# Row statistics in stages, row loads two steps ahead, left q and k in SBUF, and routing over two steps, in a recurrent attention kernel with a routed MLP

## The chip, the cores and the metric

One core of one Trainium2 chip. The metric is the device time of one execution in microseconds (us); a time below is the median of several executions. One execution of each kernel was profiled, and stage lengths come from those profiles. The profiled execution of the kernel before was long (span 2297.4 us, its median is near 2287). Steps 1 to 61, the steady steps, differ from profile to profile. Six profiles of kernels in which these steps are those of the kernel before (before, b_stats, b_qkl, b_both, b_tail, b_dn128) spread from 1974.6 to 2001.7 us, mean 1988.5; three with those of the changed kernel (after, a_again, a_route) from 1919.3 to 1941.6, mean 1929.6. The profile of the kernel before is the longest of its six, so I give the mean beside it where it matters, and read nothing from a difference under some 27 us between two profiles' steady steps.

## The reference, cut to what matters

```python
xn = layernorm(x)                       # x: [1, 2048, 1024] bf16
# A: 64 segments of 32 rows; 8 memory rows go from one segment to the next
for s in range(64):
    h = concat([mem, xn[:, 32*s:32*s+32]])           # 40 rows
    q, k, v = h @ Wq, h @ Wk, h @ Wv                 # 32 heads of 128
    o = softmax(mask(q @ k.T * scale)) @ v @ Wo
    mem = o[:, :8]; outs.append(o[:, 8:])            # recurrence
# B: the 2 rows with the largest xn @ w_r get a gated MLP (F = 3584)
r = xn @ w_r; idx = argsort(-r)[:, :2]
y = (silu(xn[idx] @ w_gate) * (xn[idx] @ w_up)) @ w_down * sigmoid(r[idx])
return x + A + (xn + scatter(y))
```

The four projections have 64 granules of 512 KB. 42 stay in SBUF; 22 must be read again in each of the 64 steps, since each segment needs the memory rows of the one before.

## The kernel before

The row statistics (mean, root of the variance) of all 2048 rows and the router sums are made during step 0, one tile of 128 rows after another. `hook(p, kc, fn)` puts a piece of work after chunk kc of phase p of a step; the phases are the six half projections (q0, k0, q1, k1, v0, v1).

```python
psT = tile_pool(name="psT", bufs=1, space=PSUM)        # ONE buffer, tag "t"
PHASES = [(0, 0), (1, 0), (0, 1), (1, 1), (2, 0), (2, 1)]
...
def stats(t):                                          # one tile in one go
    RI[t] = row_stats(pro, xt(t), P, MS[:, t, 0:1], MS[:, t, 1:2])   # DVE, Sqrt on ACT, DVE
    XN[t] = ...
    nc.gpsimd.tensor_scalar(XN[t], xt(t), MS[:, t, 0:1], subtract)
    nc.scalar.activation(XN[t], XN[t], Copy, scale=RI[t])
def router(t):                                         # DVE product with WB, sum into R
    ...
    if t == NT - 1: nc.vector.tensor_copy(out=RB, in_=R)   # frees the memory of the statistics
...
def norm(X, XN, PS, n):                                # normalize the rows of the next segment
    SC = one.tile([P, 2], F32, tag="sc", name="SC")
    nc.vector.tensor_copy(out=SC[0:n, :], in_=PS[0:n, :])  # PS is a tile of psT
    ...
def transposes(mat, half, XB):
    PTq = psT.tile([P, 4, 4, 32], BF16, tag="t", name="PTq")   # needs the same buffer
    ...
def left_keys(half):                                   # q, k of the 8 left rows, by way of HBM
    QKL[half] = load_qkl(0, half) if s == 0 else QKLs.pop(0)
...
hook(1, 1, load_rows(s + 1)); hook(3, 1, norm_rows(s + 1)); hook(4, 4, rows_st)
if s == 0:
    for t in range(1, NT): hook(*divmod(2*t - 1, 8), stats(t))
    for t in range(NT):    hook(*divmod(2*t + 1, 8), router(t))
if s == NSEG - 1:                                      # all routing in the last step
    for k, fn in zip(((0,0), (1,6), (2,0), (3,0), (4,0)), routed): hook(*k, fn)
hook(2, 5, scores(0)); hook(4, 5, scores(1))
# transposes of (q,1) come at (3, 3): two chunks after norm_rows at (3, 1)
...
# w_down: 16 loads of 2 x 112 rows, so 112 partitions each
```

## Time and profile before

| | us |
|---|---|
| median of the first 3 runs | 2284.81 (2281.93 to 2290.77) |
| profiled span | 2297.4 |
| step 0 | 138.7 |
| steps 1 to 61 | 2001.7 (32.8 each) |
| step 62, step 63 | 30.3, 46.4 |
| gate, up, down, end | 80.3 |

The stages end where ScalarE evicts the projection of a step.

### The profile page before, as it was taken

The numbers are of one execution on the slowest core, as the hardware profiler recorded it, in microseconds if no ns is written. First come the engines' busy times: TensorE is split into PE (matmuls) and PEld (weight loads), VectorE is DVE, ScalarE is ACT, GpSimd is POOL, SyncE is SP. The second block draws the span as 40 slices with busy tenths as digits, with TensorE's granted clock in tenths as the row PEclk, the third lists the DMA queues.
The fourth block names the chain that finished last, engine by engine and source line by source line (L and its number), as shares of the span: only waits on it lengthen the run. The fifth ranks groups of instructions, "written<-read, shape, count | busy, mean of one in ns | idle before, by whom it ended". The sixth has DMA issues, their size and how long they took to land.

```text
span 2297.4 us, 81760 instructions
## 1 busy us (share of the span) xinstructions
PE 1784.4 (78%) x36210; PEld 918.3 (40%) x36210; DVE 751.0 (33%) x2223; ACT 484.6 (21%) x1116; POOL 562.1 (24%) x1039
## 2 busy tenths in 40 slices
PE   2378788888888878888878888878878888887754
PEld 1134344344434444444444434444443444444321
DVE  6523233332333233323322332333223323332220
ACT  2222122212222222222212221222222122222120
POOL 6421312222131212222131222213122222222110
PEclk8589899999999899899998998898998999999967
DMA  9699999999999999999999999999999999999977
GB/s 364 213 351 388 347 363 350 379 372 364 363 357 389 347 365 368 368 372 365 380 368 361 355 376 346 370 384 350 370 348 339 387 356 388 368 374 356 382 274 232
DMA packets 294291, 818.35 MB, mean 356 GB/s; under 512 B 37520, under 2 KB 42672, under 8 KB 293936
## 3 DMA queue, kind: packets, MB, share of 16 engines
q1 hardware_dynamic: 267680, 782.33, 92.0%
q0 software_dynamic: 23936, 26.33, 3.5%
q8 instruction: 283, 4.64, 0.8%
q10 hardware_dynamic: 2320, 4.46, 0.5%
q14 instruction: 72, 0.59, 0.1%
HBM read 800.35 MB, written 12.59 MB: 354 GB/s over the span
## 4 chain that ended last, share of the span: by engine, by line
PE 41%; DMA 31%; DVE 11%; issue 8%; ACT 5%; POOL 1%; ACTq 0%; POOLq 0%; DVEq 0%; SPq 0%
PE PSm L538 19%; DMA g<-in_A_Wq_dram 16%; DMA g<-in_A_Wo_dram 6%; PE WO L576 5%; PE PSl L542 4%; DMA qkl_d<-QS 3%; PE PTq L403 3%; PE WL L576 2%; DVE SPS L450 2%; DVE NM L449 2%; ACT VM L560 2%; PE OP L490 1%; DMA g<-in_A_Wk_dram 1%; PE SPS L444 1%; ACT SPS L451 1%
## 5 line engine op out<-in xcount | busy, mean ns | idle before, releaser
L538 PE MATMUL PSm<-wres,ST 128*32 128x512 bf16 x8192 | 784.8, 419 | 20.8 <-DVE ST L298 17.9
L538 PE MATMUL PSm<-g,ST 128*32 128x512 bf16 x4096 | 443.0, 417 | 76.7 <-DMA g<-in_A_Wq_dram 53.7
L538 PEld LDWEIGHTS <-ST 128*32 128x32 bf16 x12288 | 314.4, 100 | 448.7 <-issue 210.0
L550 ACT CAST XB<-PSm 128x512 bf16<-128x512 f32 x256 | 150.2, 587 | 634.0 <-PE PSm L538 598.4
L576 PEld LDWEIGHTS <-OT 128*32 128x32 bf16 x8192 | 212.7, 98 | 78.9 <-issue 61.6
L576 PE MATMUL WO<-wres,OT 128*32 128x256 bf16 x5120 | 231.0, 278 | 12.3 <-issue 10.3
L403 PE MATMUL PTq<-IDENT,XB 128*128 128x128 bf16 x1024 | 109.0, 234 | 151.9 <-DVE SC L248 96.9
L542 PE MATMUL PSl<-wres,STL 128*32 128x512 bf16 x2048 | 215.1, 408 | 0.0
L323 POOL DMA_DIRECT2D QKL<-qkl_d x128 | 93.4, 729 | 383.2 <-PE SPS L444 155.5
L576 PE MATMUL WO<-g,OT 128*32 128x256 bf16 x3072 | 160.0, 277 | 33.9 <-DMA g<-in_A_Wo_dram 21.7
L403 PEld LDWEIGHTS <-XB 128*128 128x128 bf16 x1024 | 68.0, 102 | 258.7 <-ACT XB L550 130.5
L432 POOL COPY KT<-QKL 128x128 bf16<-128x128 bf16 x128 | 38.0, 297 | 538.6 <-PE WO L576 401.4
L609 POOL DMA_DIRECT2D out_dram<-OB x256 | 131.2, 518 | 74.6 <-DVE OB L605 35.6
L451 ACT ACTIVATE SPS<-SPS 128x320 f32<-128x320 f32 x128 | 54.0, 422 | 425.7 <-DVE SPS L450 338.6
L495 ACT CAST OT<-OP 128x256 bf16<-128x256 f32 x256 | 95.3, 372 | 209.7 <-PE OP L492 209.7
L408 DVE COPY QT<-PTq 128x512 bf16<-128x512 bf16 x128 | 53.7, 420 | 261.5 <-PE PTq L403 261.5
L490 PE MATMUL OP<-PT,VM 32*128 32x40 bf16 x2048 | 94.2, 178 | 49.9 <-ACT VM L560 45.8
L410 DVE COPY KT<-PTq 128x512 bf16<-128x512 bf16 x128 | 54.3, 424 | 208.5 <-PE PTq L403 205.6
L490 PEld LDWEIGHTS <-VM 32*128 32x128 bf16 x2048 | 65.4, 91 | 139.1 <-ACT VM L560 83.0
L497 DVE CAST OTL<-OP 128x64 bf16<-128x64 f32 x128 | 28.8, 225 | 270.1 <-ACT OT L495 270.1
L542 PEld LDWEIGHTS <-STL 128*32 128x32 bf16 x3072 | 87.2, 102 | 71.3 <-issue 21.8
L449 DVE TENSOR_REDUCE NM<-SPS 128x8 f32<-128x320 f32 x128 | 62.9, 492 | 158.7 <-PE SPS L444 158.7
(127 smaller groups left out, 2021.0 us busy)
## 6 DMA issues: line engine op xcount, KB each, us to landing
g<-in_A_Wq_dram SPq DMA_DIRECT2D x384, 512.0 KB, 7.0
g<-in_A_Wo_dram SPq DMA_DIRECT2D x384, 512.0 KB, 5.7
g<-in_A_Wk_dram SPq DMA_DIRECT2D x320, 512.0 KB, 7.2
g<-in_A_Wv_dram SPq DMA_DIRECT2D x320, 512.0 KB, 7.7
qkl_d<-QS POOLq DMA_DIRECT2D x64, 128.0 KB, 5.7
QKL<-qkl_d POOLq DMA_DIRECT2D x128, 64.0 KB, 5.8
g<-in_B_w_gate_dram SPq DMA_DIRECT2D x16, 448.0 KB, 6.0
g<-in_B_w_up_dram SPq DMA_DIRECT2D x16, 448.0 KB, 5.9
```

Source lines behind the costliest of these rows:

```text
L323: nc.gpsimd.dma_start(out=t[:, :, :], in_=qkl_d[s // 4][:, half, :, s % 4, :].rearrange("m p c -> p m c"))
L403: nc.tensor.transpose(out=PTq[:, il, :, :].rearrange("p j r -> p (j r)"), in_=XB[:, il * P:(il + 1) * P], identity=IDENT[:, :])
L410: nc.vector.tensor_copy(out=keys(half)[:, :, 0:32], in_=pv)
L449: nc.vector.tensor_reduce(out=NM[:, :], in_=S8, axis=AX.X, op=ALU.max, negate=True)
L451: nc.scalar.activation(out=S8, in_=S8, func=ACTF.Exp, scale=SCALE)
L490: nc.tensor.matmul(o, lhsT=VM[half][q0:q0 + 32, il * P:(il + 1) * P], rhs=PTm[q0:q0 + 32, il, 0:NK], start=True, stop=False, tile_position ...
L495: nc.scalar.copy(out=OT[half][:, 2 * ph:2 * ph + 2, :, :], in_=ov[:, :, :, 0:SEG])
L538: nc.tensor.matmul(PSm[32 * jq:32 * jq + 32, :], lhsT=ST[:, kc, :], rhs=Gv[:, 512 * jq:512 * (jq + 1)], start=(kc == 0), stop=(kc == KC - ...
L542: nc.tensor.matmul(PSl[32 * jq:32 * jq + 32, :], lhsT=cur["stl"][:, kc, :], rhs=Gv[:, 512 * jq:512 * (jq + 1)], start=(kc == 0), stop=(kc ...
L550: nc.scalar.copy(out=XB[:, :], in_=PSm[:, :])
L576: nc.tensor.matmul(PS[32 * g:32 * g + 32, 0:256], lhsT=lhs(h), rhs=Gv[:, D * hs + 256 * g:D * hs + 256 * (g + 1)], start=(first and hs == ...
L609: nc.gpsimd.dma_start(out=out2[s * SEG:s * SEG + XM, 256 * g:256 * (g + 1)], in_=OB[32 * g:32 * g + XM, 0:256])
```

## The change

Its intent: keep VectorE's queue flowing in step 0, so that the memory of the statistics comes free sooner; move the normalization of the next segment's rows from (3,1) to (0,4), which needs the rows loaded two steps ahead; spare the first segment's round trip of left q and k through HBM; take the router's search out of the last step; and load w_down in 128 partitions.

```diff
-    def stats(t): ...
+    def stats_a(t): ...     # DVE moments
+    def stats_b(t): ...     # Sqrt on ACT, reciprocal, subtraction on GpSimd
+    def stats_c(t): ...     # scaling on ACT, next load of x
@@ step 0
-            for t in range(1, NT):
-                hook(*divmod(2 * t - 1, 8), lambda t=t: stats(t))
             for t in range(NT):
-                hook(*divmod(2 * t + 1, 8), lambda t=t: router(t))
+                for fn, d in ((stats_a, 0), (stats_b, 1), (stats_c, 3), (router, 4)):
+                    if t > 0 or fn is router:
+                        hook(*divmod(max(2 * t - 2, 0) + d, 8), lambda t=t, fn=fn: fn(t))
@@ every step
-            hook(1, 1, ahead("x", lambda s=s: load_rows(s + 1)))
-            hook(3, 1, ahead("xn", lambda X, s=s: norm_rows(s + 1, X), "x"))
-            hook(4, 4, ahead("st", rows_st, "xn"))
+            hook(0, 4, ahead("xn", lambda s=s, X=XX[1]: norm_rows(s + 1, X)))
+            hook(1, 0, ahead("st", rows_st, "xn"))
...
+        if s + 2 < NSEG:
+            XX.append(load_rows(s + 2))            # after the residual of step s
...
-        hook(5, 2, lambda: attend(0, 0))
-        hook(5, 5, lambda: attend(0, 1))
+        hook(5, 3, lambda: attend(0, 0))
+        hook(5, 6, lambda: attend(0, 1))
@@ left q, k of step 0
+                nc.gpsimd.tensor_copy(out=first_left(half)[:, mat, :]..., in_=QS[:, 0, :, :])
...
-            QKL[half] = load_qkl(0, half) if s == 0 else QKLs.pop(0)
+            if s > 0:
+                QKL[half] = QKLs.pop(0)
@@ routing
-            for k, fn in zip(((0, 0), (1, 6), (2, 0), (3, 0), (4, 0)), routed):
-                hook(*k, fn)
+        if s == NSEG - 2:
+            hook(0, 0, routed_a); hook(3, 5, routed_b); hook(4, 0, routed_c)
+        if s == NSEG - 1:
+            hook(0, 6, routed_d); hook(2, 2, routed_e)
@@ w_down
-                nc.sync.dma_start(out=t[0:FK, :]..., in_=B_w_down[2 * what[1] * FK:(2 * what[1] + 2) * FK, :]...)
+                nc.sync.dma_start(out=t..., in_=B_w_down[2 * what[1] * P:(2 * what[1] + 2) * P, :]...)
```

Cut here: some loads of step 0 go from GpSimd's to ScalarE's queue; the hooks of the left rows move by a few chunks; routing keeps its data in one stream slot instead of two and takes the sigmoid from an exponential; silu and product of the MLP are cut in blocks of 128.

## The prediction

> **What bounds the kernel now.** I cut the run into stages first. A step is one of the 64 segments; it ends with the eviction of the projection (L604). The view of busy time by stretches, with step 0, steps 1 to 61, step 62, step 63, then gate and up, down, and the end (columns: PE, PEld, DVE, ACT, POOL busy, granted clock, DMA share, GB/s):
>
> ```profile
> 0.00:138.70 138.70, 51.27 (x692) 21.13 (x692) 71.89 (x179) 34.66 (x57) 62.50 (x60) 0.71 0.79 290
> 138.70:2140.40 2001.70, 1643.73 (x34225) 857.25 (x34225) 648.12 (x1964) 430.74 (x1021) 480.58 (x942) 0.93 0.99 366
> 2140.40:2170.70 30.30, 22.99 (x475) 11.49 (x475) 9.41 (x29) 6.17 (x16) 5.24 (x11) 0.94 1.03 404
> 2170.70:2217.10 46.40, 30.02 (x550) 16.03 (x554) 16.13 (x39) 10.33 (x21) 4.69 (x11) 0.74 0.75 255
> 2217.10:2255.20 38.10, 17.00 (x200) 5.86 (x192) 2.12 (x8) 2.75 (x5) 8.12 (x15) 0.58 0.94 359
> 2255.20:2280.00 24.80, 17.40 (x68) 5.92 (x68) 0.81 (x2) 0.00 (x0) 0.00 (x0) 0.89 1.05 282
> 2280.00:2297.40 17.40, 2.01 (x8) 0.58 (x7) 2.48 (x2) 0.00 (x0) 0.97 (x2) 0.63 0.01 2
> ```
>
> The reader is to see one bound, the weight stream: in 2002 us of steady steps the 16 DMA engines are busy 0.99 of the time, and a step takes 2001.7 / 61 = 32.8 us because 22 granules of 512 KB have to come in. Only where the share drops is there time to win: step 0 lacks 0.21 x 138.7 = 29 us of transfer time, step 63 lacks 0.25 x 46.4 = 11.6, gate and up 0.06 x 38.1 = 2.3, the end 17. The down stage is different: fully busy, yet slow.
>
> The same view inside step 0 shows where its stream stands still, and SyncE's own timeline and the chain of waits say why:
>
> ```profile
> 75.00:85.00 10.00, 6.26 (x82) 2.12 (x81) 3.25 (x9) 4.13 (x4) 3.21 (x3) 0.61 0.38 91
> 90.00:105.00 15.00, 6.02 (x56) 2.24 (x56) 12.25 (x27) 5.57 (x10) 9.19 (x4) 0.61 0.16 61
> 115.00:125.00 10.00, 4.24 (x73) 1.66 (x72) 1.48 (x3) 2.25 (x4) 2.44 (x4) 0.56 0.53 175
> ```
> ```profile
> SPq L204 <- DVE RB L159: 11.1, 1, 11.1
> ```
> ```profile
> 105.14 4.08 DMA qkl_d<-QS
> ...
> 110.20 6.19 DMA qkl_d<-QS
> ...
> 116.95 3.32 DMA QKL<-qkl_d
> ...
> 127.73 9.97 DMA wres<-in_A_Wo_dram
> ```
>
> The resident projection weights reuse the memory of the row statistics, so their loads wait for the last router sum (RB, at 105.7 us): DVE is the bound until then. After it, the first left q and k make a round trip through HBM (105 to 120 us) while PE stands.
>
> Step 63, by its timeline:
>
> ```profile
> 2182.99 2.28 DVE L342 MAX8 V<-g 1x8 f32<-1x2048 bf16 x1 [6.29 <-DMA g<-r_d]
> ...
> 2188.03 0.23 PE L439 MATMUL SPS<-KT,QT 128*32 128x40 bf16 x4 [5.45 <-DVE KT L410]
> ...
> 2198.51 0.34 PE L360 MATMUL PXS<-IDENT,g 2*128 2x2 bf16 x8 [5.09 <-DVE QT L408]
> ```
>
> The whole routing chain sits in this step. DVE waits 6.29 us for a DMA, searches for 2.28 + 2.27 us, and PE waits 5.45 and 5.09 us behind it. From the table of waits, the one that all steps share (total, times, longest):
>
> ```profile
> PE PTq L403 <- DVE SC L248: 96.9, 62, 3.8
> ```
>
> [...] The before kernel loads w_down in 112 partitions[...]. The trace has the effect: in the down stage 282 GB/s in 2 KB runs, beside 391 in a stretch with the Wo loads, which have the same 2 KB runs over 128 partitions (below). [...] the router product takes 2.01 us beside GpSimd's subtraction and 1.21 us without[...].
>
> ```profile
> DMA packets 3536, 6.77 MB, mean 282 GB/s; under 512 B 238, under 2 KB 238, under 8 KB 3535
> ```
> ```profile
> DMA packets 2400, 5.86 MB, mean 391 GB/s; under 512 B 207, under 2 KB 207, under 8 KB 2398
> ```
>
> **The change part by part.**
>
> Statistics in stages. No instruction goes away. A tile still costs DVE 1.28 (bn_stats, two) + 0.21 + 0.16 + 0.15 + 0.16 + about 2.0 (router), 4.0 us with overlaps, and the clean stretch from 25 to 40 us already runs one tile per 4.05 us. So staging doesn't speed up a tile. It removes the stalls between tiles, where DVE waited for a square root queued on ScalarE behind the scaling of a tile that GpSimd had not finished. By stretches, DVE is busy about 60 us of the 82 between 23.7 and 105.7; 22 are idle. Some idleness stays (the softmax of half 0 waits for PE and two table loads, and the square root still follows a scaling): I keep 10. The first matmul starts perhaps 1 us earlier, from 23.3, because x rows no longer queue behind mem0 on GpSimd. RB then comes at about 105.7 - 12 - 1 = 93 us.
>
> First left q and k in SBUF. Adds four GpSimd copies of some 0.3 us (the like KT copy takes 0.297), removes four round trips; the two that stalled PE cost 12.1 us (scores 0) and 9.5 us (scores 1). After RB, step 0 is then set by 15 projection granules: 7.9 MB at 375 GB/s = 21 us, plus landing and last matmuls, some 4 us. Step 0 ends near 93 + 25 = 118 instead of 138.7: **-20 us**. The two parts aren't added; the round trip lies inside that 33 us tail after RB.
>
> Routing over two steps. Step 63 loses the two DMA hops, both searches and the waits on them; it keeps a short normalization of two rows and, with the exponential in place of the sigmoid, one table load less. It should fall from 46.4 to the 32.8 to 34 of a streamed step. Step 62 takes on the search, 4.55 us of DVE, some 1 us of it seen by PE, and one stream slot of six is held for two steps instead of two for one: I give 30.3 -> 31.5. Sum: **-12 us**.
>
> Row loads two steps ahead, rows normalized at (0,4). This moves the SC wait, 96.9 / 62 = 1.56 us per step, to a place where DVE is free; the later attend hooks cut some of the 0.9 us waits on VM. PE gains up to 2 us per step, but the stream sets the step. With 0.01 of 2002 us of share to win, 20 us at most, I take half: **-10 us**. This is the least certain term.
>
> Tail. Later hooks end the 4.9 us that PE waited for the last XL rows: gate and up **-3 us**. Down in 14 loads of 128 partitions: 7.34 MB / 282 GB/s = 26.0 us becomes 7.34 / 385 = 19.1: **-7 us**. Four silus and four products in place of two each add about 1 us at the joint, beside six prefetched granules, so nothing. The last 17.4 us stay.
>
> Sum: -20 - 12 - 10 - 3 - 7 = -52; 2284.8 - 52 = **2233 us**.
>
> **Rivals.** (a) The freed waits come back as waits on the stream in all steps, as the share of 0.99 suggests: the steady term is 0, total 2243. (b) DVE's rate rules step 0: 4.05 us x 16 tiles plus the softmax leaves RB near 100, step 0 saves 12; total 2241, with (a) 2251. For it: DVE is 4.7 of 5 us busy in clean stretches. Against: the 22 idle us. (c) The steady steps are partly PE-bound: in every fourth step PE shows almost no wait for weights, and is busy 28 of 32.7 us. Then 1.5 us come off in 16 to 32 steps, another -15 to -30: 2205 to 2220. (d) The slot held for two steps starves steps 62 and 63, or the search shifts its stall into step 62: +5 to +8. (e) w_down is slow for another reason than the 112 partitions: +7.
>
> **Range and chances.** Step 0 is good to about 8 us, the steady steps to 12, the tail and routing to 5 each; together some 16, so 2212 to 2255 for 8 in 10. A gain over 2% means below 2240, 7 us from my centre: 0.63 for faster, 0.36 for same, 0.01 for slower.
>
> **What would show it.** Step 0 ending at 114 to 124 us, RB at 90 to 97, no HBM trip before the first scores; step 63 at 32 to 36 us with a share above 0.95; down near 19 us at over 370 GB/s; the SC wait nearly gone, and waits for weights up by part of it. I am wrong if RB is still after 100, if the steady steps move by over 25 us in all either way, or if step 62 grows by over 4 us.

Its sum is -20 - 12 - 10 - 3 - 7 = -52 us, so 2233 us. Moving loads from GpSimd's to ScalarE's queue is given no gain; no run tested that alone. "The effect" is that of the 112 partitions, which the prediction took for the cause without a run that showed it; b_dn128 below is that run. Each of the 8 loads of an activation table takes 1.28 us in the trace. Its 375 and 385 GB/s (the views have 366, 391 and 404) and its allowances of 4 us for landing and last matmuls and 1 us for the smaller blocks are my estimates.

## More of the kernel before

One line of the page carries what the stage table hides: the granted TensorE clock, in tenths of full speed, over 40 equal slices of the span.

```profile
PEclk8589899999999899899998998898998999999967
```

The clock reads 8 in some slices and 9 in others, all along the steady steps. A 9 means 90% or more; worked out exactly, the 34 slices that lie wholly in these steps have 0.87 to 1.00, and only two of them 1.00, so nearly every slice ran in part at half clock. Busy time at half clock is longer for the same matmuls: in a row of 128x512 matmuls the fourth after a given one starts 216 ns later at a clock of 1.00 and 427 ns later at 0.50 (medians, steps 1 to 61). So "busy" isn't a fixed amount of work here.

## The result

The changed kernel takes **2187.57 us** (median of 4 runs, 2176.01 to 2196.95), the kernel before 2286.97 us (4 runs, 2281.93 to 2290.77). The ratio is 0.9564, 95% interval 0.9514 to 0.9615, so about 99 us or 4.4% faster. A ratio is the mean time of one kernel's fast runs over the mean of the other's fast runs of the same rounds, so it is not quite the ratio of the medians. The forecast was 2233 us, a gain of 52, with a range from 2212: the direction is right, the size is outside the range.

The view of busy time by stretches, changed kernel, with the same stages and columns as the first fence of the prediction:

```profile
0.00:123.20 123.20, 50.81 (x692) 21.21 (x692) 66.91 (x179) 34.38 (x57) 57.95 (x54) 0.72 0.90 326
123.20:2064.80 1941.60, 1599.50 (x34225) 842.50 (x34225) 650.77 (x1964) 426.42 (x1021) 481.36 (x941) 0.96 1.01 378
2064.80:2094.90 30.10, 22.15 (x476) 11.24 (x476) 14.15 (x33) 6.06 (x15) 7.00 (x15) 1.00 1.00 371
2094.90:2127.00 32.10, 23.48 (x550) 13.33 (x554) 11.92 (x38) 9.03 (x20) 2.56 (x7) 1.00 1.03 402
2127.00:2160.50 33.50, 18.16 (x197) 5.52 (x188) 1.67 (x8) 2.88 (x7) 8.08 (x15) 0.62 0.99 385
2160.50:2179.00 18.50, 15.18 (x65) 5.14 (x65) 1.68 (x5) 0.00 (x0) 0.00 (x0) 0.85 1.03 392
2179.00:2195.40 16.40, 1.96 (x8) 0.49 (x6) 2.48 (x2) 0.00 (x0) 0.97 (x2) 0.62 0.01 3
```

The reader is to look at the second line. TensorE does the same 34225 matmuls as before, but in 1599.5 instead of 1643.7 us, at a mean clock of 0.96 instead of 0.93, and the stage takes 60 us less. The DMA share, 0.99 before, is now 1.01.

| stage | before | after | difference | forecast |
|---|---|---|---|---|
| step 0 | 138.7 | 123.2 | -15.5 | -20 |
| steps 1 to 61 | 2001.7 | 1941.6 | **-60.1** | **-10** |
| steps 62 + 63 | 76.7 | 62.2 | -14.5 | -12 |
| after the steps | 80.3 | 68.4 | -11.9 | -10 |

Three of four terms are near. The whole error lies in the steady steps; their difference is 59 us between the means of six and of three profiles too. Of the waits there, the tables of waits say (whole run, changed kernel; total, times, longest):

```profile
PE PTq L420 <- ACT XB L572: 67.2, 82, 6.7
...
PE PTq L432 <- DVE QT L425: 21.5, 16, 2.5
```

The wait for SC (96.9 us before) is gone, but others have grown: in steps 1 to 61 the wait for XB from 14 to 51 us, the wait for QT from 5 to 32 and the waits for weights from 87 to 111. In all, TensorE waits 330 us in these steps where it waited 349. The 19 us don't make 60. The rest is on the other side of its account: busy time fell by 44 us for the same matmuls. So the clock has to be read.

This is the view of busy time by four neighbouring stretches of 3.41 us in step 2 of the kernel before; the last three columns are the granted clock, DMA share and GB/s:

```profile
178.48:181.89 3.41, 3.41 (x85) 1.58 (x77) 1.03 (x3) 0.18 (x1) 0.96 (x2) 1.00 1.02 402
181.89:185.30 3.41, 1.20 (x21) 0.66 (x21) 3.00 (x11) 0.75 (x2) 0.08 (x1) 1.00 1.03 365
185.30:188.71 3.41, 3.41 (x31) 1.09 (x24) 0.53 (x2) 1.09 (x2) 1.22 (x2) 0.50 1.00 377
188.71:192.12 3.41, 3.20 (x75) 1.36 (x72) 1.77 (x4) 0.25 (x1) 0.71 (x1) 1.00 0.95 335
```

In the second stretch TensorE is busy for only 1.20 us, because it waits 2.21 us for SC. VectorE is busy 3.00 us of it: with the softmax of half 0 and with an eviction, behind which the small copy stands in its queue. Its timeline ends so:

```profile
184.08 0.65 DVE L554 CAST XBl<-PSl 128x512 bf16<-128x512 f32 x1
184.66 0.14 DVE L248 COPY SC<-PS 96x2 f32<-96x2 f32 x1
```

In the third stretch the clock is 0.50, and 31 matmuls fill the time in which 85 and 75 ran in the first and fourth (their mix differs somewhat). A wait of 2.2 us goes on costing after it is over: at half clock, 3.41 us hold the work of 1.7, as the 427 and 216 ns above say.

In steps 1 to 61 the kernel before has 66 such intervals of half clock, most of 3.41 us, together 272 us (266 if the one that began before is left out, as in the expectations below). For 36 of them (130 us) some of a wait for SC lies in the 3.41 us before they begin. The changed kernel has 35, together 138 us (133), none of them after such a wait. Only clocks of 0.5 and 1.0 occur in the trace, in multiples of 3.413 us but for the last interval of the run. By the 427 and 216 ns an interval at 0.5 loses half of its length: 272 x 0.5 less 138 x 0.5 is an estimate of 67 us, beside the 60 measured. That closeness is partly luck, since 272 is the highest of the six profiles (160 to 272, mean 211; the changed kernel's three have 116 to 138, mean 125). With the means the estimate is 43 of 59 us. All executions, profiled or not, say much the same: each lists its granted clock, and time x (1 - clock), the time lost to the throttle in the whole run, averages 182 us over 24 executions of the kernel before (clock 0.913 to 0.930; its profile has 0.907) and 122 us over the 10 of the changed kernel. So some 60 of the 99 to 102 us of the whole change, and some 40 of the 60 in the steady steps, are clock by this estimate.

What comes before such an interval can be counted too. Of the 65 that begin in steps 1 to 61 of the kernel before, 63 follow 3.41 us in which no single pause of TensorE reached 2.4 us; the longest pause had a median of 1.4 us. TensorE was busy for 1.69 us of those 3.41 in the median, and never for more than 2.04. In these steps of the two profiles (before, after) I cut the full-clock intervals into stretches of 3.41 us: all 20 with under 1.4 us of busy time were followed by half clock, 79 of the 170 with 1.4 to 2.2 us, and none of the 844 with 2.2 us or more.

### The profile page after: what moved, and what is told of

Same layout as the page of the kernel before. It is cut to its first block, busy times and chain, and to the rows that moved or that the text cites. A ratio compares the mean times of both kernels' runs of the same rounds, so it can differ in the third digit from the quotient of the medians.

```text
span 2195.4 us, 81816 instructions
## 1 busy us (share of the span) xinstructions
PE 1731.2 (79%) x36202; PEld 899.4 (41%) x36202; DVE 749.6 (34%) x2229; ACT 478.8 (22%) x1117; POOL 557.9 (25%) x1032
## 4 chain that ended last, share of the span: by engine, by line
PE 41%; DMA 37%; DVE 8%; issue 7%; ACT 3%; POOL 2%; ACTq 0%; SPq 0%; POOLq 0%; DVEq 0%
PE PSm L560 18%; DMA g<-in_A_Wo_dram 12%; DMA g<-in_A_Wq_dram 7%; PE WO L600 6%; PE PSl L564 6%; DMA g<-in_A_Wv_dram 5%; DMA qkl_d<-QS 5%; PE WL L600 2%; PE PTq L420 2%; DMA XL<-in_A_x_dram 2%; PE OP L509 1%; DMA QKL<-qkl_d 1%; DVE SPS L469 1%; DVE NM L468 1%; PE PTq L432 1%
## 5 line engine op out<-in xcount | busy, mean ns | idle before, releaser
L560 PE MATMUL PSm<-wres,ST 128*32 128x512 bf16 x8192 | 754.9, 398 | 23.1 <-DVE ST L300 17.8
L560 PE MATMUL PSm<-g,ST 128*32 128x512 bf16 x4096 | 421.9, 398 | 70.1 <-DMA g<-in_A_Wk_dram 31.8
L560 PEld LDWEIGHTS <-ST 128*32 128x32 bf16 x12288 | 301.2, 98 | 409.1 <-issue 164.7
L420 PE MATMUL PTq<-IDENT,XB 128*128 128x128 bf16 x1024 | 103.6, 225 | 81.1 <-ACT XB L572 67.2
L420 PEld LDWEIGHTS <-XB 128*128 128x128 bf16 x1024 | 60.2, 99 | 185.6 <-ACT XB L572 161.4
L516 DVE CAST OTL<-OP 128x64 bf16<-128x64 f32 x128 | 28.8, 225 | 284.5 <-ACT OT L514 284.5
L564 PE MATMUL PSl<-g,STL 128*32 128x512 bf16 x1024 | 106.2, 403 | 0.0
```

The source lines that it names most:

```text
L420: nc.tensor.transpose(out=PTq[:, il, :, :].rearrange("p j r -> p (j r)"), in_=XB[:, il * P:(il + 1) * P], identity=IDENT[:, :])
L560: nc.tensor.matmul(PSm[32 * jq:32 * jq + 32, :], lhsT=ST[:, kc, :], rhs=Gv[:, 512 * jq:512 * (jq + 1)], start=(kc == 0), stop=(kc == KC - ...
L564: nc.tensor.matmul(PSl[32 * jq:32 * jq + 32, :], lhsT=cur["stl"][:, kc, :], rhs=Gv[:, 512 * jq:512 * (jq + 1)], start=(kc == 0), stop=(kc ...
```

## The experiments

The kernel before was run beside each kernel on the same chip (2286 to 2288 us each time). "Half clock" is its time in steps 1 to 61 in the profile. Names that begin with b_ are edits of the kernel before, with a_ of the changed kernel. All results were correct, except b_dn128, which was wrong.

| kernel | median us | ratio to before (95%) | step 0 | 1 to 61 | 62 | 63 | rest | half clock |
|---|---|---|---|---|---|---|---|---|
| before | 2286.97 | | 138.7 | 2001.7 | 30.3 | 46.4 | 80.3 | 272 |
| after | 2187.57 | 0.9564 (0.9514 to 0.9615) | 123.2 | 1941.6 | 30.1 | 32.1 | 68.4 | 138 |
| b_norm | 2231.06 | 0.9768 (0.9702 to 0.9833) | 139.2 | 1928.2 | 29.1 | 44.5 | 79.1 | 129 |
| a_norm | 2233.83 | 0.9757 (0.9693 to 0.9820) | 121.5 | 1976.3 | 32.4 | 32.2 | 70.2 | 189 |
| b_warm | 2248.21 | 0.9838 (0.9770 to 0.9905) | 138.4 | 1953.1 | 28.8 | 45.8 | 80.1 | 68 |
| b_warm00 | 2342.25 | 1.0257 (1.0207 to 1.0306) | 139.4 | 2040.7 | 28.7 | 44.1 | 80.0 | 204 |
| b_act | 2265.38 | 0.9920 (0.9851 to 0.9989) | 141.2 | 1965.7 | 29.5 | 43.4 | 82.2 | 197 |
| a_hooks | 2204.60 | 0.9649 (0.9577 to 0.9720) | 122.5 | 1950.8 | 30.8 | 32.4 | 68.2 | 190 |
| b_stats | 2279.32 | 0.9963 (0.9947 to 0.9980) | 137.5 | 1985.9 | 29.7 | 43.8 | 79.0 | 210 |
| b_qkl | 2276.15 | 0.9960 (0.9934 to 0.9987) | 127.6 | 1982.2 | 29.1 | 44.8 | 81.8 | 205 |
| b_both | 2263.80 | 0.9901 (0.9854 to 0.9949) | 122.4 | 1996.2 | 28.9 | 43.2 | 82.0 | 199 |
| a_route | 2192.95 | 0.9620 (0.9561 to 0.9679) | 123.5 | 1919.3 | 29.5 | 43.1 | 68.3 | 116 |
| b_tail | 2277.51 | 0.9970 (0.9932 to 1.0008) | 139.4 | 1974.6 | 31.0 | 45.1 | 70.4 | 160 |
| b_dn128 | 2281.82 (1 run) | | 139.5 | 1990.4 | 30.0 | 45.5 | 75.0 | 222 |
| a_warm2 | 2173.96 | 0.9513 (0.9475 to 0.9550) | 124.2 | 1910.3 | 31.2 | 32.3 | 72.4 | 38 |
| a_again | 2182.52 | 0.9552 (0.9510 to 0.9594) | 122.8 | 1927.8 | 31.5 | 31.7 | 69.6 | 120 |
| a_warm2_5 | 2174.66 | 0.9524 (0.9480 to 0.9568) | 121.4 | 1900.5 | 30.2 | 32.7 | 72.1 | 20 |
| a_warm | 2176.15 | 0.9533 (0.9496 to 0.9570) | 123.2 | 1905.7 | 33.9 | 32.7 | 70.8 | 39 |

**My theory** for the steady steps: the stream isn't at its ceiling; the wait for SC leaves TensorE little to do in a stretch of 3.41 us (1.20 us busy in the one above), the next one runs at half clock (0.50 there), slots come free late, and the stream stands. **Rival 1:** the gain is the wait itself and has nothing to do with the clock. **Rival 2:** it comes from another part of the change (row loads two steps ahead, later hooks, other queues).

### b_norm and a_norm: the normalization of the rows alone, forward and back

```diff
 b_norm (in the kernel before)
-            hook(1, 1, ahead("x", lambda s=s: load_rows(s + 1)))
-            hook(3, 1, ahead("xn", lambda X, s=s: norm_rows(s + 1, X), "x"))
-            hook(4, 4, ahead("st", rows_st, "xn"))
+            hook(0, 4, ahead("xn", lambda s=s, X=XX[1]: norm_rows(s + 1, X)))
+            hook(1, 0, ahead("st", rows_st, "xn"))
 ... rows loaded two steps ahead
 a_norm (in the changed kernel)
-            hook(0, 4, ...norm_rows...); hook(1, 0, ...rows_st...)
+            hook(3, 1, ...norm_rows...); hook(4, 4, ...rows_st...)
```

> The kernel before with one part of the change alone: the next segment's rows are loaded two steps ahead, normalized at (0,4) and transposed at (1,0). In the trace of the kernel after, steps 1 to 61 took 1941.6 us against 2001.7 before (-60); PE busy there fell by about 74 us at the same instruction count while its waits fell by only 22, and the half-clock windows (3.41 us each) fell from 266 to 133 us in all. Clock theory: [...] moving the norm removes most of those, so steps 1 to 61 fall by 35 to 60 us, half-clock time in them below 170 us. Rival 1 (stream theory of the prediction): waits come back as waits on weights, -0 to -15 us. Rival 2 (the later attend and left hooks did it): under -15 us.

> The kernel after with the norm hook back at (3,1) and the row transposes at (4,4); rows still loaded two steps ahead. If the place of the norm is the cause, the SC wait returns (about 1.5 us per step), half-clock time returns towards 266 us and the total rises by 35 to 60 us over the kernel after, to 2222 to 2248. If the other hooks or the loads carry the gain: under +15 us.

b_norm gains 2.3% by itself, some 53 us (0.0232 x 2288; 38 to 68 by the interval): more than half of the whole change. Its steady steps by stretches:

```profile
139.18:2067.36 1928.18, 1583.82 (x34225) 843.96 (x34225) 650.25 (x1964) 432.18 (x1021) 481.75 (x942) 0.97 1.01 381
```

The same 34225 matmuls, clock 0.97, 73 us shorter than in the profile of before (60 than the mean of the six). a_norm keeps all of the change, the loads two steps ahead too, and only puts the normalization back: the wait for SC returns (98.6 us in the whole run), the half clock rises from 138 to 189 us, and its ratio is 0.9757 where the whole change has 0.9564 and 0.9552, so 44 to 47 us are lost. Both directions agree. Rival 2 falls for the larger part: it is the place of the normalization (with the transposes of its rows, which move with it in both runs), not the early loads as such.

### b_warm and b_warm00: the wait stays useful, or the same matmuls stand elsewhere

b_warm leaves the normalization late, but puts 24 matmuls with zero weights, which add zero to the open accumulation, ahead of the transposes that wait for SC. b_warm00 puts the same 24 ahead of another set of transposes, where TensorE has no such wait.

```diff
+        def warm(PS):
+            for i in range(6):
+                for jq in range(4):
+                    nc.tensor.matmul(PS[32*jq:32*jq+32, :], lhsT=MASK[:, NK:NK+SEG],      # zeros
+                                     rhs=res_tiles[0][:, 512*jq:512*(jq+1)], start=False, stop=False,
+                                     tile_position=(0, 32*jq))
 b_warm
-   ... transposes(m, h, b)
+   ... ((warm(PSm) if (m, h) == (0, 1) else None), transposes(m, h, b))
 b_warm00
+   ... ((warm(PSm) if (m, h) == (0, 0) else None), transposes(m, h, b))
```

> The kernel before, norm in its old place, so PE still can't transpose before DVE has copied SC; but 24 matmuls with zero weights (6 sets of 4, about 1.3 us) are put just before that transpose, so PE is busy in the wait. They add nothing to the sums and no work is removed. Clock theory: half-clock time in steps 1 to 61 falls from 266 us to under 190, the steps get 15 to 45 us shorter in all though PE has 1464 more matmuls. Direct-wait theory (the 1.56 us per step itself is the cost): 0 us, or 5 to 20 us longer.

> Control of b_warm: the kernel before with the same 24 zero-weight matmuls per step, but ahead of the transposes of the first block (matrix 0, half 0), where TensorE does not wait for SC. Clock theory: the half-clock time in steps 1 to 61 stays at 160 to 272 us, the wait for SC stays near 95 us, and the time is equal to the kernel before or up to 25 us above it. Rival (more matmuls raise the clock wherever they stand): a gain of 30 to 40 us as in b_warm.

Steps 1 to 61 of b_warm, then of b_warm00, by stretches:

```profile
138.41:2091.49 1953.08, 1640.60 (x35689) 877.95 (x35689) 647.33 (x1964) 430.55 (x1020) 480.75 (x942) 0.98 1.00 376
```
```profile
139.36:2180.07 2040.71, 1679.74 (x35689) 886.85 (x35689) 647.43 (x1964) 431.36 (x1021) 482.76 (x942) 0.95 0.99 360
```

And their waits for SC over the whole run:

```profile
PE PTq L409 <- DVE SC L248: 19.2, 30, 1.5
```
```profile
PE PTq L409 <- DVE SC L248: 103.7, 62, 2.2
```

This is the sharpest pair. Both do the same 35689 matmuls, 61 x 24 more than the kernel before. Ahead of the wait they make the kernel 1.6% faster, with 68 us of half clock; elsewhere 2.6% slower, with 204 us. Rival 1 doesn't survive b_warm: SC doesn't come earlier there (from the end of PS to the end of its copy the median is 2.11 us in the kernel before, in b_warm and in b_warm00), TensorE has not less to do but more, and yet the medians fall by 40 us and the stage is 49 us shorter (35 than the mean of the six profiles). That added matmuls help just by being there, whatever their place, doesn't survive b_warm00.

The pair also measures the price of TensorE time. b_warm00 loses as much to the throttle as the kernel before (180 and 182 us in the mean over all executions), so its 54 us in the median are the price of 24 matmuls per step, 0.9 us per step. A kernel bound by its stream alone would have hidden them. So in the kernel before TensorE's time was on the path. b_warm loses 113 us to the throttle, 69 less, and gains 40; by this estimate its matmuls cost some 29 us, and not 54, which fits their place: the wait for SC would have been idle time.

### b_act: the copy on another engine

```diff
-        nc.vector.tensor_copy(out=SC[0:n, :], in_=PS[0:n, :])
+        nc.scalar.copy(out=SC[0:n, :], in_=PS[0:n, :])
```

> The kernel before with SC copied by ScalarE and not by DVE, norm in its old place and rows loaded one step ahead. The wait of PE for SC should nearly vanish because ScalarE is not in the softmax chain then. If removing that wait is all that matters, by whatever means: steps 1 to 61 fall by 30 to 60 us, like b_norm. If the earlier loads or the new place of the row transposes matter: clearly less than b_norm.

It gains only 0.8%, and the table of waits says why:

```profile
PE PS L266 <- DVE QT L408: 43.5, 30, 1.6
...
PE PTq L415 <- DVE QT L408: 27.7, 17, 1.9
```

The wait for SC is gone from the steady steps (2.2 us remain there), but the next user of the single transpose buffer now waits for VectorE's QT copy instead: 71 us in all. The half clock stays at 197 us, where the six profiles have 211 in the mean; 30 of the 51 intervals that begin in these steps have some of such a wait for QT in the 3.41 us before. The wait moved, and the half clock stayed. The cause lies in VectorE's queue behind one shared buffer, and of the two ways tried only moving the work to another time cured it.

### a_hooks: the later hooks undone

```diff
-        hook(5, 3, lambda: attend(0, 0)); hook(5, 6, lambda: attend(0, 1))
+        hook(5, 2, lambda: attend(0, 0)); hook(5, 5, lambda: attend(0, 1))
 ... and the hooks of the left rows at their old places
```

> The kernel after with the attend and left-row hooks at the places they had before ((5,2), (5,5), (1,6), (3,4), (4,0), (4,2)). The waits on VM should rise from 27 to about 42 us in steps 1 to 61. If the norm's place carries the steady gain alone: total within 10 us of the kernel after (ratio 0.953 to 0.961). If the hooks carry part: 10 to 30 us longer, ratio 0.961 to 0.970.

2204.60 us against 2187.57 and 2182.52 of the changed kernel (the second, a_again, on the same chip); by the ratios, 0.9649 against 0.9564 and 0.9552, so some 19 to 22 us. They were run at other times. The time lost to the throttle over all executions is 141 us against 122. The intervals overlap a little at the edge, so take it as a likely gain, not an exact one. The wait for VM in steps 1 to 61 is 36.7 us here and 26.8 in the changed kernel; half clock 190 against 138. The forecast didn't size this by itself.

### b_stats, b_qkl, b_both: step 0 taken apart

b_stats is the kernel before with the statistics in stages alone, b_qkl with the left q and k in SBUF alone, b_both with both. The edits are the two parts of the diff above.

> The kernel before with the row statistics in stages and nothing else. In the kernel after, step 0 fell from 138.7 to 123.2 us: RB came at 97.1 us and not 105.7, and 26.1 us followed it and not 33.0. If staging is what brings RB forward, RB comes at 95 to 99 us here, but the round trip of the first q and k after it stays, so step 0 ends at 128 to 134. If it is the other order of loads on ScalarE's queue that did it, RB stays at 103 to 107. Steps 1 to 61 as before (within 15 us of 2001.7).

> The kernel before with the first left q and k kept in SBUF and nothing else. The waits of PE for the two round trips (12.1 and 9.5 us) go. If the part acts after RB as I predicted: RB within 3 us of 105.7, step 0 ends 6 to 9 us sooner, at 130 to 133. If the round trip also held up the statistics (GpSimd waits for it in order, 75 to 80 us): RB 3 to 6 us sooner as well and step 0 ends near 126.

> The kernel before with staged statistics and with q and k kept in SBUF, together. Alone they gave step 0 137.5 and 127.6 us (before 138.7), RB 105.4 and 100.9; the kernel after has 123.2 and 97.1. If staging helps only once GpSimd no longer waits in order for the round trip, the two together reach 121 to 125 and RB 96 to 99. If they only add up: 126 to 127 and RB near 100.5; then the rest of the kernel after's step 0 is the order of its first loads.

Step 0 takes 138.7, 137.5, 127.6 and 122.4 us: the stages alone give 1.2 us, SBUF alone 11.1, both 16.3. RB, after which the last resident weights can load, comes at 105.8, 105.4, 100.9 and 96.6 us. So b_stats was a miss, and the timelines show where its gain went. The kernel before, around the scores of half 0 (the square brackets hold the idle time ahead and what ended it):

```profile
76.89 0.23 PE L439 MATMUL SPS<-KT,QT 128*32 128x40 bf16 x4 [12.13 <-POOL KT L432]
...
77.77 0.49 DVE L449 TENSOR_REDUCE NM<-SPS 128x8 f32<-128x320 f32 x1 [3.65 <-PE SPS L444]
```

b_stats at the same place:

```profile
76.17 0.24 PE L450 MATMUL SPS<-KT,QT 128*32 128x40 bf16 x4 [12.78 <-POOL KT L443]
...
77.06 0.49 DVE L460 TENSOR_REDUCE NM<-SPS 128x8 f32<-128x320 f32 x1 [8.34 <-PE SPS L455]
```

The stages do make VectorE get there sooner, but its queue then holds the softmax of half 0, which waits for scores that wait for the round trip through HBM. GpSimd's queue stands behind the same trip: in b_stats it is idle for 4.48 and 3.35 us ahead of the load of q and k and of the copy KT, and its next subtraction starts only at 76.12 us. No run tells the two queues apart. The trip ends near 76 to 77 us in both kernels, so VectorE only waits longer, 8.34 us instead of 3.65. In b_both the same scores start at 67.1 us, with 4.1 us of wait ahead of them, and the stages are worth 5.2 us (127.6 to 122.4). The two parts aren't additive: the second one uncovers the first. b_both has no gain in steps 1 to 61 beyond the spread (1996.2 us), as it should have none.

### a_route: routing put back into the last step

```diff
-    at = len(flow) - 2 * n_str
+    at = len(flow) - n_str
 ... routed_a to routed_e at their places in the last step
```

> The kernel after with the routing all in the last step, as before, with one work slot, the table-free sigmoid and the new tail kept. If the place of the routing is the cause: step 63 goes from 32.1 back to 43 to 47 us, step 62 stays at 29 to 31, total +11 to +15 us. If the two work slots (now one) or the sigmoid's table load were what cost: step 63 at 34 to 39.

Step 63 goes back from 32.1 to 43.1 us, step 62 stays (30.1 to 29.5). So spreading the routing is worth 10 to 11 us of the change. The median, 2192.95 us, is 10 us above a_again's 2182.52 on the same chip, but the intervals of the ratios overlap, and the profiled steady steps happened to be 22 us shorter than in the changed kernel's profile. The stage settles it.

### b_tail and b_dn128: the MLP's end

b_tail has the new loads, blocks and hooks of the MLP alone. b_dn128 changes only the partitions of the w_down loads; it loads the wrong rows, so its result is wrong (relative error 0.148).

```diff
 b_dn128
-                nc.sync.dma_start(out=t[0:FK, :].rearrange("p (a d) -> p a d", a=2), in_=B_w_down[...112 rows, twice...])
+                r0 = min(2 * what[1] * FK, F - 2 * P)
+                nc.sync.dma_start(out=t.rearrange("p (a d) -> p a d", a=2), in_=B_w_down[r0:r0 + 2 * P, :]...)
```

> The kernel before with the tail of the kernel after (gate and up in blocks of 128 columns, w_down in 14 loads of 128 partitions, the last left rows' hooks later). The tail was 80.3 us before and 68.4 after (-11.9). If the tail's own code gives that: 67 to 71 us here, with 2 KB packets of the down stage at 84 to 90 ns and not 120.7. If a part of it came from step 63 handing over a fuller stream: 71 to 75.

> Wrong on purpose: the kernel before with its 16 w_down loads fetching 128 partitions each (a repeated stretch of rows; the matmuls still read 112), so 14 per cent more bytes and nothing else changed in the tail. If 112 partitions are what slows the 2 KB packets: 84 to 90 ns each and not 120.7, the down loads take 21 to 23 us and not 27 in spite of the extra bytes, tail 76 to 78 us. If the stage or the tensor is slow for another reason: 115 to 125 ns, tail 82 to 85.

b_tail's time doesn't separate from the kernel before (0.9970, interval across 1), but its stages after the steps take 70.4 us instead of 80.3. In b_dn128 nothing differs but the shape: 16 loads move 14% more bytes, and the stages after the steps still fall by 5.3 us, to 75.0, where the profiles with the old MLP code, b_dn128 aside, have 79.0 to 82.2. The DMA view of b_dn128 in the stretch of its down loads:

```profile
DMA packets 4312, 8.47 MB, mean 403 GB/s; under 512 B 257, under 2 KB 257, under 8 KB 4311
```

That is 403 GB/s, and the changed kernel has 392 in its down stage (the stretch from 2160.5 us above), where the kernel before had 282. A 2 KB packet of w_down takes 119.8 ns in the kernel before, 84.8 in b_dn128, 85.2 in the changed kernel. The 112 partitions were the cause. Why 112 are slow isn't shown.

### a_warm2, then a_again, a_warm2_5 and a_warm: what the clock still costs

The changed kernel still has 35 intervals of half clock in its steady steps. a_warm2 adds zero-weight matmuls ahead of its remaining long waits (8 sets of 4 where XB is waited for in steps with j = 3, 1 with j = 2, 6 ahead of the left rows' transposes with j = 2) and two sets into the scores' bank at each step's end. a_warm leaves out the latter. j is the step's number modulo 4.

```diff
+        def warm_for(what, mat, half):
+            n = {("main", 1, 1, 3): 8, ("main", 1, 1, 2): 1, ("left", 0, 1, 2): 6}.get((what, mat, half, j), 0) if s > 0 else 0
+            warm(PSm, n)
 ... a_warm2 only: 2 x 4 matmuls into SPS after the store of a step
```

> The kernel after, with zero-weight matmuls filling the longest waits of PE that are left in its steady steps: 8 sets of 4 before the transposes at (4,1) in every fourth step (2.07 us wait for ScalarE), 6 sets at (3,6) (1.34 us wait for DVE), 2 shorter sets at each step's end; no work is taken away. Clock theory: half-clock time in steps 1 to 61 falls from 133 us to under 80, and the total by 10 to 30 us below the kernel after, to a ratio of 0.943 to 0.952 of before. If the stream now is the bound in all steps: half-clock time falls but the total stays, 0.954 to 0.96.

a_again (the changed kernel), a_warm2_5 (a_warm2 again) and a_warm ran on one chip, five rounds:

> The changed kernel itself, for a comparison on one chip. Both theories: 2180 to 2197 us, 0.956 of the kernel before.

> The changed kernel with zero-weight matmuls ahead of its remaining waits, as in a_warm2. Clock theory: half-clock time stays near 38 us against some 140 of the changed kernel, and the time is 10 to 20 us below a_again (2170 to 2177 us). Rival (the streams of weights are at their ceiling in the changed kernel): equal to a_again within 5 us.

> As a_warm2_5 but without the two sets of matmuls at the end of every step; only the sets ahead of the transposes of steps with j = 2 and 3. Clock theory: between a_again and a_warm2_5, 5 to 15 us below a_again. Rival: equal to a_again within 5 us.

Steps 1 to 61 of a_warm2_5:

```profile
121.36:2021.84 1900.48, 1615.49 (x35617) 866.10 (x35613) 650.32 (x1964) 426.85 (x1021) 483.19 (x941) 0.99 1.02 386
```

The clock is 0.99 and half clock is down to 20 us, and the stream moves 386 GB/s. The means on the one chip are 2183.6 (a_again), 2173.8 (a_warm2_5) and 2177.1 us (a_warm): 9.8 us with a standard error of 5.3, and 6.5 with 4.0. That leans to the clock theory but doesn't settle it; taken with a_warm2 (0.9513) the changed kernel with these matmuls stood lower in both comparisons, by some 0.3 to 0.5%. The profile of a_warm2_5 is of its fastest execution, 2158.37 us, so the stage looks better than its median. The time lost to the throttle falls from 122 us (a_again) to 84 (a_warm2_5) in the mean over the executions, so of 38 us of clock about 10 arrive. That the added matmuls cost the rest, as b_warm00 suggests, is argued and not shown.

## Why the prediction was right or wrong

**Steady steps: wrong, and it is the step that failed.** The prediction put it: "With 0.01 of 2002 us of share to win, 20 us at most, I take half: -10 us." Two things in it were false.

First, the ceiling. I took a share of 0.99 as a full stream. A stream that doesn't stand shows 1.02 to 1.05 and about 400 GB/s (less in the down stage with its 112 partitions), since packets that overlap on one engine count twice (up to 23 are under way at once on the 16 engines): step 62 of the kernel before, in the prediction's own first fence, has 1.03 and 404 GB/s, while the steady steps have 366. At 404 GB/s the bytes of steps 1 to 61 would take 2001.7 x 366 / 404 = 1813 us, an estimate that allows 188 us to win, not 20. The best kernel here comes to 1900.5.

Second, the clock. The column stood in the same fence (0.93), and I read past it. The wait for SC was priced at its own length, 1.56 us a step, and then capped by the share. Its real price includes, in more than half of the steps, the next 3.41 us at half clock (36 such intervals in 61 steps). The runs put it at some 44 to 53 us for the place of the normalization (a_norm, b_norm), and some 20 more for the later hooks (a_hooks). Rival (c), "The steady steps are partly PE-bound", was the right one, and b_warm00 shows it directly; its "another -15 to -30" was short for the same reason. Its sum was loose, too: 1.5 us in 16 to 32 steps are 24 to 48 us, 14 to 38 beyond the 10 already counted, and 2233 less 15 to 30 is 2203 to 2218. The prediction's own alarm, "if the steady steps move by over 25 us in all either way", went off.

Over the 13 profiles without added matmuls the length of steps 1 to 61 rises by 0.56 us for each us of half clock (correlation 0.90), beside the half of the estimate above. That is a correlation, and longer waits also make half clock; the cause rests on b_warm and b_warm00. By the time lost to the throttle over all executions, b_norm has 143 us where the kernel before has 182, and a_norm 158 where the changed kernel has 122: 39 and 36 us of clock in changes of 53 and of 44 to 47. The rest is the wait itself or the stream, which no run separates.

**Step 0: near in sum (-20 forecast, -15.5 measured), in part by luck, since the working was wrong.** "It removes the stalls between tiles" was to bring RB forward by 12, "The round trip lies inside that 33 us tail after RB" was to share the tail. There were two trips, and only the second lies after RB. The first ended at 76.9 us and held up VectorE's queue and GpSimd's, so the stages alone moved RB by 0.4 us (b_stats) and the first trip's removal by 4.9 (b_qkl). RB came at 97.3 instead of 93. "I keep 10" of idle time was too little: between 23.7 us and RB VectorE is idle 73.4 - 56.5 = 16.9 us in the changed kernel, by the view of stretches. The tail after RB is 25.9 us, where the forecast had 25. SyncE's wait for the memory even grew, from 11.1 to 14.4 us, since it gets there sooner. The prediction's two figures for the router product, 2.01 us beside GpSimd's subtraction and 1.21 without, don't say all, though without consequence: in the traces of before and after a product that starts 0.12 to 0.77 us after a subtraction takes 2.07 to 1.41 us, and every other takes 1.18 to 1.23 us, those too that start 0.99 us or later into one, though subtractions are recorded for 2.83 us and more (spans on GpSimd are rough).

**Steps 62 and 63: right** (-12 forecast, -14.5 measured; step 63 at 32.1 in the forecast range of 32 to 36, share 1.03). a_route confirms 11 of it. The fear that step 62 would pay didn't come true: 30.1 us.

**After the steps: right** (-10 forecast, -11.9 measured): gate and up from 38.1 to 33.5, down from 24.8 to 18.5, the rest 1.0. The cause given for the down stage, 112 partitions, was confirmed by b_dn128; the later hooks, given for gate and up, had no run of their own.

**The parts against the whole.** b_norm 53, b_both 23, b_tail 7, a_route 11 and a_hooks some 20 make 114, beside 99 to 102 measured; with overlaps and intervals of 10 to 15 us on the larger parts that closes well enough.

**Open:** the DMA side of the same 60 us. Packets of Wo (2 KB) beyond 84 ns cost an equivalent of 50 us of all 16 engines in steps 1 to 61 before and 18 after; idle engines 62 and 42. The slow packets go with the place of the normalization (b_norm 20, a_norm 46), less with the clock alone (b_warm 39, where the six profiles with the steady steps of before have 46 to 54). No run separates whether they are a cause of part of the gain or another effect of the late normalization. What b_warm gains, it gains with some 10 us of change in them.

## What to carry to other kernels

Read the granted clock beside busy time and waits. Here all 20 full-clock stretches of 3.41 us with under 1.4 us of busy TensorE were followed by half clock, and none of the 844 with 2.2 us or more, so a wait of 1.56 us per step could cost more than its length. Moving it to a time when the engine behind it is free gained 2.3% (b_norm); giving the copy to another engine gained 0.8% (b_act). Don't take a DMA share of 0.99 as a ceiling before a stretch of the same kernel shows what a stream that never stands reaches (here 404 GB/s beside 366). When two parts of a change feed one queue, price them together: one can be worth next to nothing until the other is in (the stages 1.2 us alone, 5.2 with SBUF).
